# Moving the additions that build Winograd-style sums of weight blocks from VectorE to GpSimd

## The chip, the cores and the metric

The kernel runs on one core of one Trainium2 chip. The metric is the device time of one execution in microseconds (us). The profile names the engines PE (TensorE, matrix products), PEld (TensorE's weight loads), DVE (VectorE), ACT (ScalarE), POOL (GpSimd) and SP (SyncE, which issues nearly all DMAs). Each of them takes its instructions strictly in its own order; semaphores tell one engine that another is done.

## The reference

Random-feature attention, and behind it a two-layer network over all 4608 tokens, all in float32:

```
phi(x): h = x @ omega.T - |x|^2/2;  exp(h - max h) / sqrt(m)      # m = 128 features
kv = sum_s phi(k)[s] outer v[s];  z = sum_s phi(k)[s]             # for each of 8 batches, 8 heads
x  = (phi(q) @ kv) / (phi(q) . z + 1e-6)                          # 4608 tokens x 512
h  = x @ w_in;  g = h * tanh(softplus(h))                         # 512 x 2048
out = g @ w_out                                                   # 2048 x 512
```

## The kernel before

Matrix products run in float16. A float32 operand is kept as a high part (its cast to float16) and a low part (what the cast lost, again as float16), and three products (low by high, high by low, high by high) stand for one. The function `cast` (L71) makes a high part, `rest` (L80) a low part; a low part is one instruction that reads the float32 source and the high part, both from SBUF.

**The stages.** The tokens are worked in 18 chunks of 256. The attention for later tokens (`k_task`, `q_task`) is spread as small steps over the network's products for earlier chunks: an agenda hands out one step of each running task per slot, between groups of `ff_in` (x by w_in, tiles `ph`) and `ff_out` (g by w_out, tiles `po`). So PE gets a steady mixture of `ph`, `po`, `pk`/`pq` (features), `pkv` and `pn`.

**The sums.** The last three chunks (15 to 17, `ff_in7` and `ff_out7`) need seven products of blocks where the plain way needs eight. For that they use sums and differences of weight blocks, which `sums_make` (L797) prepares long before. It runs eight times: `t_make` four times for w_out (float32 scratch tile `sw`, results `t_w`, DRAM tiles `dt_w`), then `s_make` four times for w_in (scratch tile `s`, results also `s`, DRAM tiles `ds`). One call makes four results. Its ten additions and subtractions go through the local function `tt` (L805): two sums of blocks and a third that adds them, then result 1 is sent; two more, result 2 is sent; two more, result 3; three more, result 4. Each is 128x512 with a float32 output, and reads weight blocks in float16 or the scratch tile in float32. "Sent" (`send`, L808) is a cast on ACT, a low part on DVE and a DMA to DRAM. The fourth addition writes over the scratch that result 1's low part still reads, so it waits for that low part on DVE; likewise the eighth waits for that of result 2 and the ninth for that of result 3.

**What sets the order.** The agenda gives the order in which instructions are recorded; a scheduler then orders each engine's instructions by its own estimate of when they could start. So a change of engine moves neighbours too. What the prediction's steps touch, besides: the maximum of the features and its subtraction (L426, L435, DVE, out of PSUM), the exponential on ACT (L441, behind a table load), the cast and low part of `kp` and `qn` (ACT and DVE), the low part of `g` (L85, DVE), and on POOL the low parts `sk`, `sq` (of k and q), `vb` (of v) and `xs` (of x). `pkv` (L522) is the product on PE that reads `kp` and `vb`.

Of the kernel before, what the change touches and what calls it, by code (L numbers as in the profile page):

```python
# [30 lines left out]
def tile_kernel(  # L31
# [37 lines left out]
    act, dve, pool = nc.scalar, nc.vector, nc.gpsimd  # L69

    def cast(eng, out, in_, scale=1.0):  # L71

        if eng is act:
            act.activation(out, in_, AF.Copy, scale=scale)  # L74
        elif isinstance(scale, float) and scale == 1.0:
            eng.tensor_copy(out, in_)  # L76
        else:
            eng.tensor_scalar_mul(out, in_, scale)

    def rest(eng, out, in_, hi, scale=1.0):  # L80

        if isinstance(scale, float) and scale == 1.0:
            eng.tensor_tensor(out=out, in0=in_, in1=hi, op=ALU.subtract)  # L83
        else:
            eng.scalar_tensor_tensor(  # L85
                out=out, in0=in_, scalar=scale, in1=hi, op0=ALU.mult, op1=ALU.subtract
            )
# [177 lines left out]
    def did(*key):  # L265
        done[key] = done.get(key, 0) + 1

    def must(n, *key):
        assert done.get(key, 0) >= n, key
# [527 lines left out]
    def sums_make(key, blocks, first, shape):  # L797
        n = BW // 2
        must(1, "s", 0, NB - 1)
        must(1, "s", 1, 0)  # L800
        t = sb.tile([P, 2, n], F32, tag="ht", name=f"s{key[0]}_{key[1]}", bufs=HB)
        s, u = (t[:, i].rearrange("p (a b) -> p a b", a=shape) for i in range(2))
        b11, b12, b21, b22 = blocks

        def tt(out, in0, in1, op=ALU.subtract):  # L805
            dve.tensor_tensor(out=out, in0=in0, in1=in1, op=op)

        def send(op, src):  # L808
            o = sb.tile([P, 2, n], F16, tag="xs", name=f"{op}_{key[0]}_{key[1]}", bufs=2)
            cast(act, o[:, 0], src)  # L810
            yield 1
            rest(dve, o[:, 1], src, o[:, 0])
            sums[key[0], key[1], op] = dram.tile([P, 2, n], F16, name=f"d{op}_{key[0]}_{key[1]}")
            nc.sync.dma_start(out=sums[key[0], key[1], op], in_=o)
            yield 1

        ops = ("s1", "s2", "s4", "s3") if first is ALU.add else ("t1", "t2", "t4", "t3")
        tt(s, b22(0) if first is ALU.add else b12(0), b21(0) if first is ALU.add else b11(0), first)
        yield 1
        tt(u, b22(1) if first is ALU.add else b12(1), b21(1) if first is ALU.add else b11(1), first)  # L820
        yield 1
        tt(s, s, u, ALU.add)
        yield from send(ops[0], t[:, 0])
        if first is ALU.add:
            tt(s, s, b11(0))
            yield 1
            tt(s, s, b11(1))
        else:
            tt(s, b22(0), s)
            yield 1  # L830
            tt(s, s, b22(1), ALU.add)
        yield from send(ops[1], t[:, 0])
        last = b12 if first is ALU.add else b21
        tt(u, last(0), s)
        yield 1
        tt(u, u, last(1), ALU.add)
        yield from send(ops[2], t[:, 1])
        pair = (b11, b21) if first is ALU.add else (b22, b12)
        tt(s, pair[0](0), pair[1](0))
        yield 1  # L840
        tt(u, pair[0](1), pair[1](1))
        yield 1
        tt(s, s, u, ALU.add)
        yield from send(ops[3], t[:, 0])
        did("sums" if first is ALU.add else "tsums")
# [500 lines left out]
```

## Time and profile before

| | |
|---|---|
| time, median of 3 runs | 941.36 us (940.48 to 941.49) |
| the profiled execution's own time | 939.57 us |
| its span, first to last instruction | 937.8 us |
| mean granted TensorE clock | 0.993 |
| PE busy | 920.5 us (98%) |
| PEld busy | 689.4 us (74%) |
| DVE busy | 707.1 us (75%), 1234 instructions |
| ACT busy | 658.9 us (70%) |
| POOL busy | 213.6 us (23%), 134 instructions |
| DMA | 108.69 MB, mean 116 GB/s |
| the 80 instructions at L806 | 64.85 us on DVE, between 275 and 720 us |

A span is the time from the first to the last instruction; what lies around it in the profiled execution is 939.57 - 937.8 = 1.77 us. Busy time counts instructions that an engine executes; waiting before an instruction is not in it, but waiting inside one (for a port of the memory, say) is. In a timeline row the first number is the start in us from the span's beginning, the second the length in us, then engine, source line, operation, out<-in, shape and count; in brackets stands the engine's idle time before it and who ended it. A row that ends in x2 merges two instructions.

### The profile page before, as it was taken

The page shows a single profiled execution, that of the slowest core. Times are in us where ns is not written, and L with a number is a line of the kernel's source. Part 1 is how long each engine was busy: PE and PEld are TensorE (multiplying, and loading weights), DVE is VectorE, ACT ScalarE, POOL GpSimd, SP SyncE. Part 2 cuts the span into 40 slices and gives each one's busy share as a digit, 9 for nine tenths or more (in the row PEclk, how much of TensorE's full clock was granted, in tenths as well). Part 3 has the DMA queues.
Part 4 walks back from the last instruction along what each step waited for, and adds up shares of the span by engine and source line. Part 5 has one row for each costly group of instructions (what it writes and reads, how often), then busy time and mean ns, then how long its engine had stood idle before and what let it go on. Part 6 is the DMA issues. An engine that isn't in the chain of part 4 may idle for free. (4 is left out here: it accounts for less than half of the span.)

```text
span 937.8 us, 21111 instructions
## 1 busy us (share of the span) xinstructions
PE 920.5 (98%) x8795; PEld 689.4 (74%) x8795; DVE 707.1 (75%) x1234; ACT 658.9 (70%) x873; POOL 213.6 (23%) x134
## 2 busy tenths in 40 slices
PE   9799989999999999999999999999999999999998
PEld 6688765677777777777777777777777777679997
DVE  5799898685678688787688857878688756658774
ACT  6568966678777878778677776788786866345442
POOL 0000023242342224321333134231241232200000
PEclk9799999999999999999999999999999999999999
DMA  9766325443442256323543265523533156973521
GB/s 308 264 227 215 108 58 93 99 83 75 95 107 85 80 115 128 90 81 76 107 114 97 69 120 107 126 60 93 112 73 91 35 114 141 210 218 92 162 66 45
DMA packets 153055, 108.69 MB, mean 116 GB/s; under 512 B 112832, under 2 KB 125248, under 8 KB 152960
## 3 DMA queue, kind: packets, MB, share of 16 engines
q1 hardware_dynamic: 152640, 106.75, 44.6%
q8 instruction: 69, 1.13, 0.5%
q10 hardware_dynamic: 320, 0.59, 0.2%
q14 instruction: 26, 0.21, 0.1%
HBM read 63.14 MB, written 17.83 MB: 86 GB/s over the span
## 5 line engine op out<-in xcount | busy, mean ns | idle before, releaser
L770 PE MATMUL ph<-xT,w 128*128 128x256 f16 (+1 forms) x2816 | 342.2, 278 | 0.0
L1097 PE MATMUL po<-wo,g 128*128 128x512 f16 x1344 | 308.5, 379 | 0.0
L770 PEld LDWEIGHTS <-w 128*128 128x128 f16 x2688 | 260.7, 98 | 46.1 <-issue 0.6
L1097 PEld LDWEIGHTS <-g 128*128 128x128 f16 x1344 | 127.2, 98 | 132.7
L83 POOL TENSOR_TENSOR sq<-fq,sq 64x1024 f16<-64x1024 f32 x31 | 70.5, 2275 | 253.6 <-ACT sq L74 177.8
L955 ACT ACTIVATE h<-ph,us 128x512 f32<-128x512 f32 (+3 forms) x152 | 83.2, 573 | 49.7 <-PE ph L770 48.5
L85 DVE SCALAR_TENSOR_TENSOR g<-h,us,g 128x1024 f16<-128x1024 f32 (+3 forms) x76 | 99.9, 1325 | 15.2 <-ACT g L74 14.9
L83 POOL TENSOR_TENSOR sk<-fk,sk 64x1152 f16<-64x1152 f32 x24 | 59.3, 2469 | 91.6 <-ACT sk L74 79.3
L83 POOL TENSOR_TENSOR xs<-x,xs 128x512 f16<-128x512 f32 (+1 forms) x35 | 40.7, 1164 | 153.0 <-DVE xs L76 102.0
L955 ACT ACT_TABLE_LOAD x56 | 71.8, 1283 | 1.0
L441 ACT ACT_TABLE_LOAD x53 | 68.0, 1283 | 4.2 <-DVE ek L435 3.3
L426 DVE TENSOR_REDUCE mxq<-pq 128x4 f32<-128x512 f32 x72 | 46.7, 682 | 24.8 <-PE pq L401 23.9
L83 DVE TENSOR_TENSOR qn<-eq,qn 128x1024 f16<-128x1024 f32 x31 | 39.2, 1263 | 29.9 <-ACT qn L74 29.9
L906 PEld LDWEIGHTS <-w 128*128 128x128 f16 x1008 | 59.0, 98 | 3.3 <-issue 0.7
L441 ACT ACTIVATE ek<-ek,lnt 128x1152 f32<-128x1152 f32 x24 | 30.1, 1256 | 42.3 <-DVE ek L435 42.2
L74 ACT ACTIVATE g<-h,us 128x1024 f16<-128x1024 f32 (+3 forms) x64 | 58.2, 932 | 0.8
L426 DVE TENSOR_REDUCE mxk<-pk 128x4 f32<-128x512 f32 (+1 forms) x96 | 49.5, 546 | 7.3 <-PE pk L416 3.5
L83 DVE TENSOR_TENSOR kp<-ek,kp 128x1152 f16<-128x1152 f32 x24 | 32.8, 1366 | 27.0 <-ACT kp L74 26.2
L1044 PEld LDWEIGHTS <-gb 128*128 128x128 f16 x504 | 48.3, 98 | 5.2
L83 POOL TENSOR_TENSOR vb<-vf,vb 128x640 f16<-128x640 f32 x24 | 37.3, 1554 | 55.2 <-DVE vb L76 41.5
L955 ACT ACTIVATE h<-h,us 128x1024 f32<-128x1024 f32 (+2 forms) x16 | 14.7, 930 | 48.6 <-DVE h L915 48.6
L441 ACT ACTIVATE eq<-eq,lnt 128x1024 f32<-128x1024 f32 x31 | 35.6, 1149 | 18.8 <-DVE eq L435 18.5
(185 smaller groups left out, 1370.3 us busy)
## 6 DMA issues: line engine op xcount, KB each, us to landing
w<-ds SPq DMA_DIRECT2D x48, 256.0 KB, 3.6
vf<-in_vL_dram SPq DMA_DIRECT2D x32, 325.0 KB, 3.3
out_dram<-o SPq DMA_DIRECT2D x36, 256.0 KB, 2.3
fq<-in_qT_dram SPq DMA_DIRECT2D x31, 256.0 KB, 3.5
fk<-in_kT_dram SPq DMA_DIRECT2D x24, 256.0 KB, 3.6
raw<-in_w_out_dram SPq DMA_DIRECT2D x5, 1024.0 KB, 7.8
wo<-in_w_in_dram SPq DMA_DIRECT2D x4, 1024.0 KB, 10.6
raw<-in_w_in_dram SPq DMA_DIRECT2D x4, 1024.0 KB, 15.3
```

What stands on the lines that cost most here:

```text
L74: act.activation(out, in_, AF.Copy, scale=scale)
L83: eng.tensor_tensor(out=out, in0=in_, in1=hi, op=ALU.subtract)
L85: eng.scalar_tensor_tensor(out=out, in0=in_, scalar=scale, in1=hi, op0=ALU.mult, op1=ALU.subtract)
L426: sub = dve.tensor_reduce(out=mx[:, lo:hi], in_=pp[:, :m, :], axis=AX.X, op=ALU.max, negate=by_act)
L441: last = act.activation(e, e, AF.Exp, bias=lnt)
L770: nc.tensor.matmul(out=ph[:, i, :], lhsT=wi(a, k, f) if c else wi0(k, f), rhs=xT[c][:, y, k, :] if c else xT0()[:, k, :], start=n == 0, st ...
L906: nc.tensor.matmul(out=ph[:, i, :], lhsT=left(gr, op_l, i, a, k), rhs=x_region(c, r)[:, y, k0 + k, :], start=n == 0, stop=n == len(mm) - 1,)
L955: act.activation(h[:, :, lo:hi], ph[:, :, lo:hi], AF.Mish, scale=us[:, 0:1])
L1044: nc.tensor.matmul(out=ps, lhsT=gT[c, n][:, i, a, f, :], rhs=rhs, start=f == 0 and (a, y) == (1, 0), stop=f == FG - 1 and (a, y) == (0, 0),)
L1097: nc.tensor.matmul(out=po[i], lhsT=gT[c, gr][:, a, f % FG, i * P:(i + 1) * P], rhs=wo(y, f), start=f == 0 and (a, y) == parts[0], stop=f = ...
```

## The change

The ten additions and subtractions of each `sums_make` are issued to GpSimd instead of VectorE. Casts stay on ScalarE, low parts on VectorE, DMAs on SyncE's queue.

```diff
@@ sums_make
         def tt(out, in0, in1, op=ALU.subtract):
-            dve.tensor_tensor(out=out, in0=in0, in1=in1, op=op)
+            pool.tensor_tensor(out=out, in0=in0, in1=in1, op=op)
```

80 instructions leave DVE and 80 come to POOL. PE keeps its instructions in the same order; the other queues are reordered around the sums. The place shown here is the first call of `s_make` (scratch tile `s_0_6511`, made of weight slots `w_102` and `w_104`), about 512 to 550 us into the span. On POOL, between the low parts of v and of q, before and now in one (lines with + are new):

```order
 L83 TENSOR_TENSOR vb_116<-vf_3_5413,vb_116 128x10x64
+L806 TENSOR_TENSOR s_0_6511<-w_104 128x512 x2
+L806 TENSOR_TENSOR s_0_6511<-s_0_6511 128x512
+L806 TENSOR_TENSOR s_0_6511<-s_0_6511,w_102 128x512 x2
+L806 TENSOR_TENSOR s_0_6511<-w_102,s_0_6511 128x512
+L806 TENSOR_TENSOR s_0_6511<-s_0_6511,w_102 128x512
+L806 TENSOR_TENSOR s_0_6511<-w_102,w_104 128x512
 L83 TENSOR_TENSOR sq_6624<-fq_6509,sq_6624 64x1024
+L806 TENSOR_TENSOR s_0_6511<-w_102,w_104 128x512
+L806 TENSOR_TENSOR s_0_6511<-s_0_6511 128x512
 L83 TENSOR_TENSOR sq_6753<-fq_6667,sq_6753 64x1024
```

Eight sums stand ahead of the low part `sq_6624`, two behind it; the fourth, the eighth and the ninth each wait for a low part on DVE.

On DVE, in the same stretch (`s_0_0_6575` is result 1 of the call, `s_0_0_6683` result 2; `mxk_3` is the maximum for the k features of the fourth pair of heads, whose exponential becomes `kp_3`):

```order
-L806 TENSOR_TENSOR s_0_6511<-w_104 128x512
 L83 TENSOR_TENSOR kp_2_6343<-ek_2_6233,kp_2_6343 128x1152
-L806 TENSOR_TENSOR s_0_6511<-w_104 128x512
 L319 TENSOR_REDUCE vmx_8502<-vf_0_8366 128x1
-L806 TENSOR_TENSOR s_0_6511<-s_0_6511 128x512
 L83 TENSOR_TENSOR s_0_0_6575<-s_0_6511,s_0_0_6575 128x512
-L806 TENSOR_TENSOR s_0_6511<-s_0_6511,w_102 128x512
+L83 TENSOR_TENSOR s_0_0_6683<-s_0_6511,s_0_0_6683 128x512
 L426 TENSOR_REDUCE mxk_3_6399<-pk_3_0_6400 128x4
 L426 TENSOR_REDUCE mxk_3_6399<-pk_3_4_6409 128x1
```

The sums are gone, and the low part of result 2, which stood behind `kp_3` before, now stands ahead of `mxk_3`, right behind the low part of result 1.

On ACT, in the same stretch (`s_0_0_6846` is result 3; `ek_3` is the exponential, the line above it its table load):

```order
 L74 ACTIVATE s_0_0_6575<-s_0_6511 128x512
+L74 ACTIVATE s_0_0_6683<-s_0_6511 128x512
 L955 ACTIVATE h_0_0_6314<-ph_0_0_2_6373,us_6308 128x512
 L74 ACTIVATE g_0_6313<-h_0_0_6314,us_6308 128x1024
 L74 ACTIVATE sq_6624<-fq_6509 64x1024
+L74 ACTIVATE s_0_0_6846<-s_0_6511 128x512
 L74 ACTIVATE kv_5680<-pkv_2_6433 128x2x65
 L441 ACT_TABLE_LOAD
 L441 ACTIVATE ek_3_6398<-ek_3_6398,lnt 128x1152
+L74 ACTIVATE kp_3_6502<-ek_3_6398 128x1152
 L955 ACT_TABLE_LOAD
 L955 ACTIVATE h_0_1_6473<-ph_0_1_0_6474,us_6308 128x512
```

The casts of results 2 and 3 moved up, ahead of the exponential, and the cast `kp_3` now follows the exponential directly instead of standing behind the next table load.

## Prediction

> **What bounds the kernel now.** I read the page first: which engine is full.
>
> ```profile
> span 937.8 us, 21111 instructions
> ## 1 busy us (share of the span) xinstructions
> PE 920.5 (98%) x8795; PEld 689.4 (74%) x8795; DVE 707.1 (75%) x1234; ACT 658.9 (70%) x873; POOL 213.6 (23%) x134
> ```
>
> PE is busy for 920.5 of 937.8 us and no other engine for more than 75%. An average says little of the stretch in question, so the table by stretches comes next, with the cuts put where the sums (L806) begin and end.
>
> ```profile
> 0.00:275.00 275.00, 262.63 (x2161) 196.07 (x2162) 215.73 (x388) 204.34 (x315) 57.99 (x47) 0.98 0.54 147
> 275.00:720.00 445.00, 444.74 (x4215) 320.16 (x4214) 347.44 (x593) 339.29 (x403) 130.48 (x70) 1.00 0.40 96
> 720.00:938.00 218.00, 213.12 (x2423) 173.17 (x2421) 143.96 (x255) 115.32 (x156) 25.15 (x17) 1.00 0.46 118
> ```
>
> In 275 to 720 us PE is busy for 444.74 of 445.00 us at a full granted clock (1.00), while DVE is busy for 347.44 us (78%), ACT for 339.29 and POOL for 130.48 (29%). PE is the bound there and lacks 0.26 us. A view of waits says what PE waited for; this is its whole answer for PE's matrix products from 275 to 900 us, in us, times and longest.
>
> ```profile
> PE p_s L906 <- DVE h L915: 0.6, 1, 0.6
> PE pn L572 <- DMA qp<-qn: 0.5, 1, 0.5
> PE pn L572 <- DVE ek L435: 0.3, 1, 0.3
> ```
>
> 1.4 us in all, of which 0.3 lie before 720. One more wait is put down to PE's weight loads:
>
> ```profile
> PEld L522 <- DVE kp L83: 0.4, 1, 0.4
> ```
>
> So DVE's work between 275 and 720 us is not on the path that sets the end, except through such short waits. The change can gain next to nothing; what it can lose is the margin by which DVE, ACT and POOL run ahead of PE.
>
> **What is removed.** The sums on DVE, as a row of the table by stretches for L806 alone:
>
> ```profile
> 275.00:720.00 445.00, 64.85 (x80) 1.00 0.40 96
> ```
>
> 80 instructions, 64.85 us, all beside a busy PE: price on the path 0. DVE would come down to 347.44 - 64.85 = 282.6 us (64%). What an earlier DVE could win is PE's waits, 1.4 us at most or 0.15%, and most of these lie behind the last sum.
>
> **What is added.** 80 sums on POOL. No row has POOL read float16 blocks and write float32, so the nearest rows set the price: POOL's own two-input instructions, by size, mean ns of one behind the comma.
>
> ```profile
> L83 POOL TENSOR_TENSOR xs<-x,xs 128x512 f16<-128x512 f32 x32 | 38.4, 1200 | 140.2 <-DVE xs L76 89.2 <-issue 38.8 <-ACT xs L74 11.6
> L83 POOL TENSOR_TENSOR vb<-vf,vb 128x640 f16<-128x640 f32 x24 | 37.3, 1554 | 55.2 <-DVE vb L76 41.5 <-DVE rd L583 4.6 <-DVE vam L330 4.5
> L83 POOL TENSOR_TENSOR xs<-tt,xs 128x512 f16<-128x512 f32 x3 | 3.5, 1154 | 0.7 <-DVE xs L76 0.7
> L83 POOL TENSOR_TENSOR xs<-x,xs 128x256 f16<-128x256 f32 x3 | 2.3, 772 | 12.8 <-DVE xs L76 12.8
> ```
>
> 128x512 takes 1154 to 1200 ns; I take 1.15 us for a sum. Float16 inputs could make it cheaper, 0.77 us (the row with half the elements), or dearer, 1.55 us (a quarter more elements). 80 x 1.15 = 92 us bring POOL from 130.5 to 222.5 of 445 us, 50%: POOL does not become the bound.
>
> **What POOL and DVE do to each other.** Two pieces of the timeline. In the first a low part of `g` on DVE, with two inputs in SBUF, begins beside a low part on POOL:
>
> ```profile
> 495.72 2.37 POOL L83 TENSOR_TENSOR sk<-fk,sk 64x1152 f16<-64x1152 f32 x1 [6.46 <-ACT sk L74]
> 495.93 3.24 DVE L85 SCALAR_TENSOR_TENSOR g<-h,us,g 128x1024 f16<-128x1024 f32 x1
> ```
>
> POOL ends at 498.09; DVE's instruction ends 1.08 us later, at 499.17. It had stood still for 2.16 us. In the second DVE waits while POOL has more work ready:
>
> ```profile
> 577.99 1.34 POOL L83 TENSOR_TENSOR xs<-x,xs 128x512 f16<-128x512 f32 x1 [4.09 <-DVE xs L76]
> 578.24 0.80 DVE L319 TENSOR_REDUCE vmx<-vf 128x1 f32<-128x640 f32 x1
> 578.97 1.45 DVE L85 SCALAR_TENSOR_TENSOR g<-h,us,g 128x1024 f16<-128x1024 f32 x1
> ...
> 579.29 2.38 POOL L83 TENSOR_TENSOR vb<-vf,vb 128x640 f16<-128x640 f32 x1
> ```
>
> DVE's `g` (578.97) waits for the end of `xs` at 579.33 and ends at 580.42; `vb`, already begun, then needs until 581.67, 1.0 us longer than its mean. So the two take turns, a whole instruction each, and DVE waits for one POOL instruction at most. A sum on POOL thus costs a DVE instruction of that kind up to 1.15 us. If each of the 80 did, DVE would have 282.6 + 92 = 374.6 us, 84% of the stretch: dearer than now, and still not a bound. The Trainium skill, "Perfetto Trace Analysis", section on optimizing Scalar and DVE operations, speaks against the change: moving operations between these two engines might not help because they share a port. The rows agree that they block each other; by that rule the DVE relief would be smaller than 64.85 us, which the sum, with relief at 0, can do without.
>
> **What moves: the waits in line.** A queue in order can hold up work that has nothing to do with the sums. I looked for each call of `sums_make` at what stands between the results in the new order. In most calls DVE and ACT have work of their own between the results; in the last one the low part of result 4 stood ahead of the next maximum before too. I put these at 0; that is judged by the starts of their rows, not worked out for each. The first call of `s_make` is different: DVE's new order has the low part of result 2 directly behind that of result 1 and ahead of `mxk_3`. Between the two stand sums 4 and 5 on POOL and a cast on ACT, and DVE and ACT must wait for them. In the trace of before, POOL there:
>
> ```profile
> 511.45 1.41 POOL L83 TENSOR_TENSOR vb<-vf,vb 128x640 f16<-128x640 f32 x1 [2.23 <-DVE vb L76]
> 520.71 2.12 POOL L83 TENSOR_TENSOR sq<-fq,sq 64x1024 f16<-64x1024 f32 x1 [7.85 <-issue]
> ```
>
> DVE (maximum, subtraction, `g`, last subtraction, and the low part `kp` that PE wants):
>
> ```profile
> 517.91 0.69 DVE L83 TENSOR_TENSOR s<-s,s 128x512 f16<-128x512 f32 x1 [0.70 <-ACT s L74]
> 518.64 0.69 DVE L806 TENSOR_TENSOR s<-s,w 128x512 f32<-128x512 f32 x1
> 519.25 0.88 DVE L426 TENSOR_REDUCE mxk<-pk 128x4 f32<-128x512 f32 x2
> 520.05 0.88 DVE L435 TENSOR_TENSOR ek<-pk,mxk 128x512 f32<-128x512 f32 x2
> 520.84 0.68 DVE L426 TENSOR_REDUCE mxk<-pk 128x4 f32<-128x512 f32 x1
> 521.44 2.47 DVE L85 SCALAR_TENSOR_TENSOR g<-h,us,g 128x1024 f16<-128x1024 f32 x1
> 523.84 0.68 DVE L435 TENSOR_TENSOR ek<-pk,mxk 128x512 f32<-128x512 f32 x1
> ...
> 528.89 1.36 DVE L83 TENSOR_TENSOR kp<-ek,kp 128x1152 f16<-128x1152 f32 x1 [2.13 <-ACT kp L74]
> ```
>
> ACT (cast of result 1, exponential, cast of `kp`):
>
> ```profile
> 517.25 0.63 ACT L74 ACTIVATE s<-s 128x512 f16<-128x512 f32 x1 [1.84 <-DVE s L806]
> ...
> 524.55 1.26 ACT L441 ACTIVATE ek<-ek,lnt 128x1152 f32<-128x1152 f32 x1 [2.50 <-DVE ek L435]
> ...
> 527.71 1.15 ACT L74 ACTIVATE kp<-ek 128x1152 f16<-128x1152 f32 x1
> ```
>
> and PE's product, which needs `kp` complete (528.89 + 1.36 = 530.25), 0.81 us later:
>
> ```profile
> 531.06 1.12 PE L522 MATMUL pkv<-vb,kp 128*128 128x65 f16 x30
> ```
>
> Worked through with these lengths: `vb` ends at 512.86; three sums and one turn for DVE's `kp` of the heads before (1.36) end at 512.86 + 3.45 + 1.36 = 517.7, the cast 0.63 later at 518.3, the low part at 519.0 (before: 518.60). Sums 4 and 5 end at 521.3, the cast of result 2 at 521.9; its low part waits out sum 6 to 522.4 and ends at 523.1. Only then does `mxk_3` start, 3.9 us later than at 519.25. From it to `g` are 521.44 - 519.25 = 2.2 us: 525.3. `g` waits out sum 8 (525.4); `sq`, which held it until 522.83 before (1.4 of its 2.47 us), now comes behind it. It takes 1.1 more, and the last subtraction ends at 527.2, against 523.84 + 0.68 = 524.5. The exponential ends at 528.5, and the cast of `kp`, now directly behind, at 529.6 (before: 528.86). The low part of `kp` meets the low part of result 3 and the ninth sum; it ends between 531.0 (nothing in the way) and 531.9 (one sum, 1.15, in the way). PE wants it at 531.06. So PE waits 0 to 0.9 us; I take 0.7. With a sum of 0.77 us the wait is gone; with 1.55 us about seven sums on this way add 0.4 each, 2.8 us, and the wait is 3.5 us. The cover that hides all the rest is PE's backlog; where it is gone a late sum costs its lateness in full, but once, since while PE waits the others catch up.
>
> DMAs: each result's store to DRAM comes with its low part, a few us earlier or later in SyncE's queue; the results are read again some 100 us later or more, so 0.
>
> **Sum.** 0 for the removed work, 0 for the added, +0.7 for the one wait: 939.57 + 0.7 = 940.3 for the profiled execution. The runs' median stands 941.36 - 939.57 = 1.8 above that execution, so 942.1 is the forecast of the median. A difference below 0.2% (1.9 us) can hardly be told from none for this kernel: its own three runs spread over 0.1%.
>
> **The rivals.** First, slower: ACT and DVE stand in line behind POOL. The place is the stretch above, 517 to 532 us, and the price goes by the length of a sum: seven on the way, 0.7 us of wait at 1.15. To cost more than 1.9 us a sum must take (1.9 - 0.7) / 7 = 0.17 us more, 1.32 us. At 1.55 it costs 3.5 us: 944.9. For it: a `vb` of 128x640 already takes 1.55 on average, and DVE's turns lengthen the series. Against it: the rows with the sums' own shape lie at 1.15 to 1.20.
>
> Second, faster: the relief of DVE wins. DVE's `ek` and `kp` (rows above, 0.3 and 0.4) come earlier, since sums that stood ahead of them are gone. All 1.4 us gone gives 940.0, which is still no measurable change; for more, PE would have to run faster than it does, and no row shows room for that.
>
> Third, much slower: the work is simply on the worse engine. If every one of the eight calls makes PE wait for one whole sum, that is 8 x 1.15 = 9.2 us: 950.6. Against it: PE's margin in most calls is more than a sum. The Trainium skill, "GPSIMD Engine Reference", section on engine selection, sends elementwise additions to VectorE because GpSimd is about twice as slow for two inputs; the rows agree (64.85 / 80 = 0.81 us on DVE with its waits, 1.15 on POOL), but speed counts only where PE waits for it.
>
> **How the numbers follow.** The forecast has 0.62, the first rival 0.27, the second 0.07, the third 0.04. The second ends beyond 0.2% only if more than PE's known idle time goes: 0.03 for faster. Same is 0.62 + 0.04 = 0.66, slower 0.27 + 0.04 = 0.31. The range reaches down to the second rival, rounded to 940.1, and up past the first with 0.6 us for a second place of its kind, to 945.5.
>
> **What would show it.** Right: DVE busy some 40 to 65 us less and POOL some 92 more, L806 rows on POOL at about 1.15 us, PE still near 444 of 445 us in the stretch, and a wait of `pkv` for `kp` of under 1 us near 531. Wrong: waits of PE on `kp`, `ph`, `pn` or `po` of several us in sum between 275 and 720 (first or third rival), sums of 1.4 us or more, or ACT idle before casts of `s` and `t_w` for much longer than now with PE waiting behind it.

## The result and the profile after

The changed kernel takes 949.34 us (median of 4 runs, 947.55 to 951.95) against 940.92 us of the kernel before in the same comparison (4 runs, 938.77 to 941.49): a ratio of 1.0093, with a 95% interval of 1.0075 to 1.0111. It is slower by 0.9%, 8.4 us. The profiled execution took 948.67 us with a span of 946.9, 9.1 us more than that of before. The forecast was 942.1 us, with a range of 940.1 to 945.5.

The page's line of busy times, for the changed kernel:

```profile
PE 923.6 (98%) x8795; PEld 691.0 (73%) x8795; DVE 671.3 (71%) x1154; ACT 658.8 (70%) x873; POOL 329.5 (35%) x214
```

DVE lost 707.1 - 671.3 = 35.8 us of busy time and POOL gained 329.5 - 213.6 = 115.9, where 92 were forecast. The stretch of the sums in the table by stretches, with the same columns as before (busy time of PE, PEld, DVE, ACT and POOL, each with its number of instructions, then the granted clock, the DMA share and GB/s):

```profile
275.00:720.00 445.00, 440.57 (x4179) 317.51 (x4177) 305.35 (x505) 335.79 (x398) 240.87 (x148) 1.00 0.41 94
```

Between 275 and 720 us PE is idle for 4.43 us where it was idle for 0.26. And here is what PE's matrix products waited for from 275 to 900 us (us, times, longest):

```profile
PE pkv L522 <- DVE kp L83: 4.7, 3, 2.1
PE pk L401 <- DVE ek L435: 1.6, 1, 1.6
PE pn L572 <- DMA qp<-qn: 0.9, 1, 0.9
```

7.2 us instead of 1.4, in five places. So PE is the bound as before, and what hides the rest has holes. The sums themselves, first as the row of the table by stretches for L806 alone, then their largest group (shortest, median and longest in ns):

```profile
275.00:720.00 445.00, 111.24 (x79) 1.00 0.41 94
L806 POOL TENSOR_TENSOR sw<-wo x16: 1146/1242/2273, 275.2 to 498.3; 128x512 f32<-128x512 f16 x16
```

111.24 / 79 = 1.41 us on average: from 1.15 us, as forecast, with a median of 1.24 in this group, up to 2.27 where an instruction of DVE has to be let through (the sum at 287.54 below takes 2.15 us).

**Where the 9.1 us lie.** PE executes the same instructions in the same order in both kernels, so the lateness of one and the same product tells when time was lost. The first `pkv` product of five groups of heads, before:

```profile
197.85 1.12 PE L522 MATMUL pkv<-vb,kp 128*128 128x65 f16 x30
...
304.26 1.12 PE L522 MATMUL pkv<-vb,kp 128*128 128x65 f16 x30
...
427.56 1.12 PE L522 MATMUL pkv<-vb,kp 128*128 128x65 f16 x30
...
494.02 1.12 PE L522 MATMUL pkv<-vb,kp 128*128 128x65 f16 x30
...
725.75 1.13 PE L522 MATMUL pkv<-vb,kp 128*128 128x65 f16 x30
```

and after:

```profile
199.13 1.12 PE L522 MATMUL pkv<-vb,kp 128*128 128x65 f16 x30
...
308.16 1.00 PE L522 MATMUL pkv<-vb,kp 128*128 128x65 f16 x26 [0.69 <-DVE kp L83]
...
433.35 0.90 PE L522 MATMUL pkv<-vb,kp 128*128 128x65 f16 x13 [2.15 <-DVE kp L83]
...
501.29 1.12 PE L522 MATMUL pkv<-vb,kp 128*128 128x65 f16 x30
...
734.99 1.13 PE L522 MATMUL pkv<-vb,kp 128*128 128x65 f16 x30 [1.85 <-DVE kp L83]
```

The rows with x26 and x13 are cut off by the end of their view. The lateness is 1.28, 3.90, 5.79, 7.27 and 9.24 us. The first 1.28 lie ahead of the first sum: the profiled execution of before had begun quickly (in the ten other kernels' profiles below this product comes 0.72 to 2.25 us later than at 197.85). Then the first `t_make` costs 2.62 us. Before has a short wait near 381 (0.26 us of PE's idle time) that the changed kernel has not, which wins 0.43 us of lateness back, and the third `t_make` costs 2.31. Between 434 and 500 another 1.48 are lost with no wait: the granted clock fell behind that third place, told at the end. The last `s_make` costs 1.97. 1.28 + 2.62 - 0.43 + 2.31 + 1.48 + 1.97 = 9.23. The place that the prediction had worked through, the first `s_make`, costs nothing here.

**The first and the third `t_make`.** A timeline of the changed kernel in the first, put together from POOL, SyncE, DVE, ACT and PE in the order of time:

```profile
287.54 2.15 POOL L806 TENSOR_TENSOR sw<-sw,wo 128x512 f32<-128x512 f32 x1
289.66 1.40 POOL L83 TENSOR_TENSOR vb<-vf,vb 128x640 f16<-128x640 f32 x1
291.09 0.34 SPq L306 DMA_DIRECT2D vf<-in_vL_dram  x1
293.84 0.82 DVE L319 TENSOR_REDUCE vmx<-vf 128x1 f32<-128x640 f32 x1 [5.16 <-DMA vf<-in_vL_dram]
...
296.09 1.28 DVE L83 TENSOR_TENSOR t_w<-sw,t_w 128x512 f16<-128x512 f32 x2
...
300.88 0.63 ACT L74 ACTIVATE t_w<-sw 128x512 f16<-128x512 f32 x1 [8.15 <-POOL sw L806]
...
303.53 0.68 DVE L435 TENSOR_TENSOR ek<-pk,mxk 128x512 f32<-128x512 f32 x1
...
304.26 0.62 PE L401 MATMUL pk<-om,sk 128*128 128x128 f16 x8 [1.60 <-DVE ek L435]
```

and the rows of before that answer to them:

```profile
283.12 1.40 POOL L83 TENSOR_TENSOR vb<-vf,vb 128x640 f16<-128x640 f32 x1 [2.30 <-DVE vb L76]
284.55 0.34 SPq L306 DMA_DIRECT2D vf<-in_vL_dram  x1
287.20 0.82 DVE L319 TENSOR_REDUCE vmx<-vf 128x1 f32<-128x640 f32 x1 [1.34 <-DMA vf<-in_vL_dram]
...
291.68 0.63 ACT L74 ACTIVATE t_w<-sw 128x512 f16<-128x512 f32 x1 [2.35 <-issue]
...
295.98 0.68 DVE L435 TENSOR_TENSOR ek<-pk,mxk 128x512 f32<-128x512 f32 x1
```

Read down: four sums, the last of them at 287.54, stand on POOL ahead of the low part `vb`, which starts at 289.66 instead of 283.12 (1.28 of these 6.54 us are from before the first sum). `vb` is the last reader of a float32 tile `vf` (L305, five buffers), and the fetch of a later `vf` into that buffer waits for it: it is issued at 291.09, 0.03 us behind the end of `vb` (291.06), instead of 284.55. On DVE the maximum `vmx` over that fetch (L319) stands in line, though PE reads what is made of it only at 353.60. DVE is idle for 5.16 us in front of it, where it waited 1.34 before. Behind it stand two low parts `t_w`; POOL's last three sums wait for these; ACT's cast of the fourth result waits for the sums (8.15 us, at 300.88; in before the cast at this place of ACT's line is that of the second result, at 291.68), and the fourth result's low part stands on DVE ahead of the last subtraction `ek`, at 303.53 against 295.98; the exponential on ACT comes behind both. PE's backlog is used up: it waits 1.60 us for that subtraction and 0.69 us for `kp`. In the third `t_make` the same rows read 414.01 for `vb`, 415.44 for the fetch, 419.23 for `vmx` with an idle time of 6.20 us, and PE waits 2.15 us.

**The last `s_make`.** In the changed kernel the cast and the low part of result 4, and `kp`:

```profile
722.13 0.63 ACT L74 ACTIVATE s<-s 128x512 f16<-128x512 f32 x1 [3.62 <-POOL s L806]
722.80 1.21 DVE L83 TENSOR_TENSOR s<-s,s 128x512 f16<-128x512 f32 x1 [2.85 <-ACT s L74]
...
733.57 1.36 DVE L83 TENSOR_TENSOR kp<-ek,kp 128x1152 f16<-128x1152 f32 x1 [3.50 <-ACT kp L74]
```

and before:

```profile
713.56 1.07 DVE L83 TENSOR_TENSOR s<-s,s 128x512 f16<-128x512 f32 x1 [0.74 <-ACT s L74]
...
724.34 1.36 DVE L83 TENSOR_TENSOR kp<-ek,kp 128x1152 f16<-128x1152 f32 x1 [3.50 <-ACT kp L74]
```

The order on DVE is the same in both: the low part, the next maximum, `kp`. But the low part now ends a chain of POOL's sums, ACT's casts and DVE's low parts, and comes 9.24 us later. 7.27 of them PE is late itself. In before `kp` ended at 724.34 + 1.36 = 725.70, and PE used it at 725.75: there was no margin. So PE pays the remaining 9.24 - 7.27 = 1.97 us in full.

### The profile page after: what moved, and what is told of

It reads as the page before. It is cut to its first block, busy times and chain, and to the rows that moved or that the text cites. A ratio compares the mean times of both kernels' runs of the same rounds, so it can differ in the third digit from the quotient of the medians.

```text
span 946.9 us, 21117 instructions
## 1 busy us (share of the span) xinstructions
PE 923.6 (98%) x8795; PEld 691.0 (73%) x8795; DVE 671.3 (71%) x1154; ACT 658.8 (70%) x873; POOL 329.5 (35%) x214
## 5 line engine op out<-in xcount | busy, mean ns | idle before, releaser
L85 DVE SCALAR_TENSOR_TENSOR g<-h,us,g 128x1024 f16<-128x1024 f32 (+3 forms) x76 | 102.9, 1363 | 18.6 <-ACT g L74 18.4
L83 POOL TENSOR_TENSOR sk<-fk,sk 64x1152 f16<-64x1152 f32 x24 | 61.6, 2566 | 55.9 <-ACT sk L74 44.5
L83 DVE TENSOR_TENSOR qn<-eq,qn 128x1024 f16<-128x1024 f32 x31 | 42.4, 1366 | 35.3 <-ACT qn L74 35.3
L83 DVE TENSOR_TENSOR kp<-ek,kp 128x1152 f16<-128x1152 f32 x24 | 37.7, 1572 | 24.6 <-ACT kp L74 24.6
```

The costliest lines, as they stand in the source:

```text
L85: eng.scalar_tensor_tensor(out=out, in0=in_, scalar=scale, in1=hi, op0=ALU.mult, op1=ALU.subtract)
```

## The experiments

The theory formed from these rows was named the **late-fetch theory**, with a second place of its own at the last `s_make`. Its rivals: the **port theory** (POOL's sums hold up DVE's instructions, and the loss is spread over all of them), the **round-trip theory** (a result's way over three engines makes ACT and DVE stand in line, whatever the fetch), and the prediction's own (one place, the first `s_make`). The times of each set are compared with runs of the kernel before beside them, whose medians were 940.37, 940.28, 940.15 and 940.26 us.

The helper `behind(name)` in the diffs, which the kernel has already, queues what stands in its block behind the last instruction kept under that name, on the same engine and without a wait. TensorE's order is the same in all ten kernels.

**Which calls lose.** Two kernels divide the calls; the upper new line is the first, the lower the second.

```diff
-            pool.tensor_tensor(out=out, in0=in0, in1=in1, op=op)
+            (dve if first is ALU.add else pool).tensor_tensor(out=out, in0=in0, in1=in1, op=op)
+            (pool if first is ALU.add else dve).tensor_tensor(out=out, in0=in0, in1=in1, op=op)
```

The first kernel, with the sums of `t_make` alone on GpSimd:

> The sums of the four t_make calls on GpSimd, those of the four s_make calls on VectorE as before. Late-fetch theory (in the first and third t_make the sums stand ahead of the low part vb on GpSimd, which holds the buffer that the next vf is fetched into; VectorE's maximum vmx waits in order for that fetch, and the exponential and kp behind it come late): the places in these two calls stay, 1.8 + 0.9 us near 302 to 307 and 2.3 us near 431, and those after the s_make calls go: about 5 us over before, 945.9. Theory of the prediction (one place, the first s_make, and a place of that kind elsewhere only by chance): no more than before, 940.9. Port theory (every sum on GpSimd holds up VectorE, and the loss is spread over all sums): 44 of 80 sums stay, 8.4 x 44 / 80 = 4.6, 945.5, but spread over all four calls instead of two places.

Measured: 945.63 us (944.36 to 946.91), ratio 1.0053 (1.0041 to 1.0065), 5.3 us. PE's waits in its trace from 275 to 720 us are those of the two calls, 1.6 for `ek` and 2.6 for `kp`:

```profile
PE pkv L522 <- DVE kp L83: 2.6, 2, 1.9
PE pk L401 <- DVE ek L435: 1.6, 1, 1.6
```

The second kernel, with the sums of `s_make` alone on GpSimd:

> The reverse: the sums of the four s_make calls on GpSimd, those of t_make on VectorE. Late-fetch theory: what is left is the wait after the last s_make, about 2 us of kp near 728, and up to 1 us of pn near 792: 943.0 to 944.0. Theory of the prediction, with dearer sums of 1.3 to 1.4 us: PE waits for kp near 531, 2 to 3 us, and the whole loss is here, 949.3. Port theory: 36 of 80 sums, 8.4 x 36 / 80 = 3.8, 944.7, spread over the four calls.

Measured: 944.38 us (943.68 to 945.36), ratio 1.0039 (1.0027 to 1.0051), 4.0 us, a little above the 943.0 to 944.0 of the late-fetch theory. The two halves make 5.3 + 4.0 = 9.3 us. The wait behind the last `s_make` is there (1.86 us). Two others were not in the changed kernel's trace: one at the first `s_make`, and one that nothing had foretold:

```profile
533.46 1.13 PE L522 MATMUL pkv<-vb,kp 128*128 128x65 f16 x30 [0.48 <-DVE kp L83]
...
604.58 0.92 PE L572 MATMUL pn<-kv,qp 128*128 128x65 f16 x24 [1.72 <-DMA qp<-qn]
```

The first is the place of the prediction, at half a microsecond. In the changed kernel it is hidden: there `kp` is complete at 537.76, 4.36 us later than in this kernel, but PE comes to it at 538.33, 4.87 us later. The second is taken up below. The expectations count 44 sums for `t_make` and 36 for `s_make`; it is 40 each, which gives the port theory 4.2 us for either half. The two times, 5.3 and 4.0, do not refute it, but the places do: 4.2 of the 5.3 us are waits at two calls.

**Is it the fetch?** One kernel moves the maximum `vmx` alone.

```diff
-        yield 3 if b else 6
+        yield 3 + 1 * (b == 6) if b else 6
...
-            with behind(AV if b == 0 else None, 1):
+            with behind("dlo" if (b, hp) in ((4, 3), (6, 0)) else AV if b == 0 else None, 0 if b else 1):
...
-            yield 0 if hp % 2 == 0 or b == 0 else 1
+            yield 1 if (b, hp) == (4, 2) else 0 if (b, hp) in ((4, 3), (6, 1)) else 0 if hp % 2 == 0 or b == 0 else 1
...
-        anchors[nth] = (last.ins, sub.ins)
+        anchors[nth] = (last.ins, sub.ins); anchors["dlo"] = (sub.ins,)
```

`dlo` is the last subtraction of features that was written out. The shift by one step keeps that of the later steps.

> The changed kernel, with the maximum vmx of two fetches (the ones that VectorE waited for 5.2 us near 291 and 6.2 us near 413) queued some 50 places later on VectorE; TensorE's, ScalarE's, GpSimd's and SyncE's orders are the same, sums and low parts vb stay as late as they were. Late-fetch theory: VectorE goes on with the low parts, the exponential and kp come in time, and the 4.9 us of TensorE's waits at 302 to 307 and 431 go: 949.3 - 4.9 = 944.4. Round-trip theory (the casts and low parts of each result make ScalarE and VectorE stand in line behind GpSimd, whatever the fetch): not changed, 949.3. Port theory: not changed, 949.3.

Measured: 944.93 us (942.77 to 947.72), ratio 1.0050 (1.0034 to 1.0066): 4.4 us less than the changed kernel, 4.9 forecast. The fetch is issued as late as it was (SyncE, the first row), and yet PE waits in neither `t_make` (the second fence has all its waits from 275 to 900 us):

```profile
291.27 0.34 SPq L306 DMA_DIRECT2D vf<-in_vL_dram  x1
...
291.71 1.28 DVE L83 TENSOR_TENSOR t_w<-sw,t_w 128x512 f16<-128x512 f32 x2
```
```profile
PE pn L572 <- DMA qp<-qn: 2.2, 2, 1.8
PE pkv L522 <- DVE kp L83: 1.9, 1, 1.9
```

What is left of `pkv` is the last `s_make`, and `pn` is the unforetold wait near 600. The low parts `t_w` start at 291.71 instead of 296.09. The sums, the way of the results and the port are as in the changed kernel, so the round-trip and the port theory fall for these two calls: it is DVE's wait in line for the late fetch. The interval of this kernel and that of the change (1.0075 to 1.0111) do not meet.

**Is it the low part behind the sums?** One kernel moves POOL's line instead.

```diff
-            eng.tensor_tensor(out=out, in0=in_, in1=hi, op=ALU.subtract)
+            return eng.tensor_tensor(out=out, in0=in_, in1=hi, op=ALU.subtract)
...
-        rest(by("vlo", nth), v_lo, va, v_hi, s_v)
+        anchors["vlo"] = (rest(by("vlo", nth), v_lo, va, v_hi, s_v).ins,)
...
-            pool.tensor_tensor(out=out, in0=in0, in1=in1, op=op)
+            with behind("vlo"): pool.tensor_tensor(out=out, in0=in0, in1=in1, op=op)
```

> The changed kernel, with each sum of a weight block queued on GpSimd behind the last low part vb that was written out before it: in the first t_make vb then stands ahead of sums 4 to 7, in the third ahead of three of these four; TensorE's order is the same. Late-fetch theory: the fetch is issued as early as before, vmx does not wait, and 2.6 us of the first call and most of 2.3 of the third go: 944.4 to 945.5. Round-trip theory: the results' way from GpSimd over ScalarE and VectorE is as long in the third call as it was, so its 2.3 us stay and only the first call's may go: 946.7 to 949.3. Port theory: the same sums hold up VectorE as often, 949.3.

Measured: 943.01 us (941.41 to 946.36), ratio 1.0033 (1.0020 to 1.0045): 6.3 us less than the changed kernel, more than the 4 to 5 forecast (its profile has no wait near 600 and no fall of the clock either). In the first `t_make` `vb` stands ahead of sum 4 and `vmx` waits 0.47 us:

```profile
285.35 1.41 POOL L83 TENSOR_TENSOR vb<-vf,vb 128x640 f16<-128x640 f32 x1 [1.71 <-DVE vb L76]
...
289.57 0.82 DVE L319 TENSOR_REDUCE vmx<-vf 128x1 f32<-128x640 f32 x1 [0.47 <-DMA vf<-in_vL_dram]
```

In the third call the results go as long a way as before, with `vb` at 407.66 and a wait of 0.57 us for `vmx`, and PE waits nowhere. What is left of PE's waits for `kp` is that behind the last `s_make`:

```profile
PE pkv L522 <- DVE kp L83: 1.9, 1, 1.9
```

**The last `s_make`.** To the kernel just told, one more line, with the exponential's instruction kept under `exp`:

```diff
-            cast(act, o[:, 0], src)
+            with behind("exp" if op == "s3" and key == (1, 1) else None): cast(act, o[:, 0], src)
```

> The changed kernel with vb first, as in the run before, and the cast and the low part of the last result of the last s_make queued behind the next exponential on ScalarE and some 20 places later on VectorE; the sums and their order on GpSimd are the same. Theory of the line (this cast and low part come at the end of nine sums in a chain, 3.5 us later than on VectorE, and the maximum, the exponential and kp stand behind them): the wait of 2.0 us for kp near 727 goes, 943.0 - 2.0 = 941.0, that is the time of before within its spread. Port theory (the sums hold up VectorE itself): not changed, 943.0.

Measured: 941.86 us (939.04 to 943.80), ratio 1.0012 (0.9999 to 1.0024): no difference from before that the runs can tell, and 0.9 over the forecast (the turn told below is still open in this kernel). The median is 1.15 us under that of the fourth kernel, but the two intervals meet; what shows the place is the trace, in which no wait for `kp` is left. The sums on GpSimd are as they were, so here it is the line and not the port.

**Controls.** The sums of `t_make` alone, with the order behind `vb` of the fourth kernel:

> Only the sums of t_make on GpSimd, behind the low part vb; those of s_make on VectorE. Late-fetch theory: nothing is left of the 5.3 us that these calls cost with vb behind the sums: 940.4. Round-trip or port theory: 44 sums on GpSimd still cost 2 to 5 us: 942.4 to 945.6. Were the relief of VectorE worth anything (about 35 us less work), it would show here as a time under before, 939.5 or less.

Measured: 940.08 us (938.58 to 943.48), ratio 1.0001 (0.9991 to 1.0012). And the second and fourth `t_make` alone on GpSimd, with no order set:

```diff
+            (pool if key in (("w", 1), ("w", 3)) else dve).tensor_tensor(out=out, in0=in0, in1=in1, op=op)
```

> Only the sums of the second and the fourth t_make on GpSimd, the others on VectorE, with no order set by hand. Late-fetch theory: in these two calls no fetch that VectorE waits for hangs on a low part behind the sums, so nothing is lost: 940.4. Port theory: 22 of 80 sums, 8.4 x 22 / 80 = 2.3: 942.7. Round-trip theory: the results of these calls go the same way as those of the first and third, 2 to 3 us: 942.4 to 943.4.

Measured: 940.25 us (939.21 to 943.35), ratio 0.9999 (0.9991 to 1.0008). These 20 sums cost nothing, as the theory has it for calls in which no awaited fetch hangs on a low part behind them, though their results go the same way over three engines (for 20 sums, not 22, the port theory gives 2.1 us, which the interval excludes). PE's row between 275 and 720 us is full in both; the first is the kernel with all of `t_make`, the second that with two calls:

```profile
275.00:720.00 445.00, 445.00 (x4222) 320.79 (x4220) 327.51 (x554) 342.15 (x408) 189.17 (x111) 1.00 0.40 96
```
```profile
275.00:720.00 445.00, 445.00 (x4222) 320.75 (x4220) 337.36 (x574) 342.67 (x407) 159.74 (x91) 1.00 0.39 96
```

**The wait near 600.** In the second kernel it goes with a turn between DVE and POOL. DVE's low part `g` and POOL's `sk` start within 0.12 us of each other:

```profile
587.60 2.36 POOL L83 TENSOR_TENSOR sk<-fk,sk 64x1152 f16<-64x1152 f32 x1 [3.92 <-issue]
587.72 3.32 DVE L85 SCALAR_TENSOR_TENSOR g<-h,us,g 128x1024 f16<-128x1024 f32 x1
```

`g` came second and took 3.32 us, and what stands behind it on DVE, up to the low part `qn` that PE's `pn` needs by way of `qp`, is late. Two more kernels have the sums of `s_make` alone on GpSimd. In one only the very last result is moved, as above:

> Only the sums of s_make on GpSimd, with the cast and the low part of the very last result queued behind the next exponential (as in the run that did this to the changed kernel). Theory of the line: the 2.0 us of kp near 728 go, those of pn near 603 (1.9) and of kp near 533 (0.65) stay: 944.4 - 2.0 = 942.4. Port theory: not changed, 944.4.

Measured: 942.73 us (940.26 to 944.76), ratio 1.0020 (1.0009 to 1.0031). The median is where it was forecast, but the profiled execution, 941.26 us, has no wait near 603. The order on each engine at this place is that of the second kernel; this time `g` won the turn, by 0.16 us, and `sk` waited:

```profile
587.18 1.28 DVE L85 SCALAR_TENSOR_TENSOR g<-h,us,g 128x1024 f16<-128x1024 f32 x1
587.34 3.35 POOL L83 TENSOR_TENSOR sk<-fk,sk 64x1152 f16<-64x1152 f32 x1 [3.93 <-DVE vmx L319]
```

Six of the profiles have this order, with `g` and `sk` 0.03 to 0.16 us apart. In two `g` comes second, and PE waits 1.72 us (second kernel) and 1.77 us (third). In four it comes first, and PE waits nowhere near 600: the changed kernel, the fourth, the fifth and this one. Of the eleven times of this kernel six lie above 942.5 us, of the twelve of the next one two; this suggests that one program goes either way from execution to execution, but no two traces of one program show it. The other kernel queues the maximum ahead of `g` later, so that `g` can start well ahead of `sk`:

```diff
-            with behind(AV if b == 0 else None, 1):
+            with behind("dlo" if (b, hp) == (7, 2) else AV if b == 0 else None, 0 if b else 1):
```

> As the kernel before it, and the maximum vmx that VectorE waits for 5.0 us near 582 queued some 80 places later, so that the low part g that stood behind it starts ahead of GpSimd's low part sk and need not stand still behind it (g took 3.32 us there, against 1.27 where it came first). If that lost turn makes the wait of 1.9 us for qp near 603: 942.4 - 1.9 = 940.5, and g takes about 1.3 us. If it is the results' way over three engines in the second s_make: the wait stays, 942.4.

Measured: 940.58 us (939.83 to 942.72), ratio 1.0009 (1.0000 to 1.0018), and `g` took 1.44 us at 580.59, 5.65 us ahead of `sk`. This edit also takes `g` out from behind DVE's wait of 5.0 us for a fetch. That this wait alone is not the cause is shown by the six profiles: DVE waits 4.7 to 5.0 us there in all of them.

**All of it together**: the changed kernel, all 80 sums on GpSimd, with these three orders.

> All 80 sums on GpSimd as in the changed kernel, with the three orders of the runs before together: sums behind vb, the very last result behind the next exponential, and the maximum vmx near 582 queued later. If these three places and the first s_make's half microsecond are the whole of the loss: 940.2 + 0.6 - 0.4 (TensorE's own wait near 381, which went in most of the other runs) = 940.4, no difference from before, and TensorE busy for 445 of 445 us. If 80 sums on GpSimd cost something more that the runs of parts did not show: 942 or more. If the relief of VectorE by 36 us of busy time can bring something once nothing waits: under 938.3.

Measured: 940.10 us (939.18 to 944.50), ratio 1.0007 (0.9996 to 1.0018). Its stretch, and all of PE's waits to 900 us:

```profile
275.00:720.00 445.00, 445.00 (x4220) 320.49 (x4218) 314.02 (x513) 342.56 (x406) 246.64 (x150) 1.00 0.41 95
```
```profile
PE pn L572 <- DMA qp<-qn: 0.3, 1, 0.3
PE p_s L906 <- DVE h L915: 0.2, 1, 0.2
```

As far as the runs can tell (the interval ends at 0.18%, 1.7 us), the places of these three orders are the whole of the loss. Nor does PE wait at the first `s_make`: `kp` is complete at 530.83 and PE comes at 531.34. DVE's relief brings nothing that the runs can tell, even with these waits gone. None of the ten kernels is faster than the one before.

## Why the prediction was wrong

**What was right.** PE is the bound; the relief of DVE is worth 0 (last experiment: DVE busy for 674.3 us instead of 707.1, and no time won). 80 sums on POOL need not cost anything by themselves. Most sums alone take what the nearest row said, 1.15 us (1.26 where both inputs lie in the scratch tile). POOL and DVE take turns by whole instructions: the rows near 587 us above show both outcomes, with 3.32 us for the loser in one profile (`g`) and 3.35 us in the other (`sk`). The Trainium skill, "SBUF — State Buffer", section on SBUF's two separate sides, describes this as an exclusive lock that whoever starts first holds for the whole instruction, and these rows agree. DVE's busy time in the whole run fell by 35.8 us and not by the 64.85 that left it: its other instructions became 29 us longer together. The place that was worked out was also sized rightly: 0.7 us forecast at the first `s_make`, 0.48 measured in the second kernel, where nothing ahead of it had cost PE time. This was not luck, for the steps in between fit as well: from the start of `vb` to that of `mxk_3` the working has 523.1 - 511.45 = 11.65 us, and the second kernel and the changed one both take 11.66; to the end of `kp` it has 19.6 to 20.5, and they take 20.2. It did not show in the change itself because PE was late by then: "while PE waits the others catch up".

**The step that failed** is this one: "In most calls DVE and ACT have work of their own between the results; in the last one the low part of result 4 stood ahead of the next maximum before too. I put these at 0; that is judged by the starts of their rows, not worked out for each." Three of the other seven calls were not 0 but 2.62, 2.31 and 1.97 us, and the fall of the clock behind the second of these three cost 1.48 more in the profiled execution. For the last call the observation itself was right and the conclusion wrong. That an instruction already stood ahead of the maximum says nothing for the cover when that instruction becomes later; the new chain of sums, casts and low parts in front of it had to be added up as was done for the first `s_make`.

For the two `t_make` calls the reason lies in a link that the prediction left out. "DMAs: each result's store to DRAM comes with its low part, a few us earlier or later in SyncE's queue; [...] so 0" speaks of the DMAs of the moved step alone (and of the reading of the results 100 us later, which does not hold for all: in before the first `w<-ds` is issued at 520.64, 2.01 us behind the first store; no loss in the runs hangs on it). But the sums were also put ahead of `vb` on POOL, and `vb` sets free the buffer of a fetch. With that the fetch came 6.5 us later (291.09 against 284.55). The link itself could be seen in before's trace: the fetch at 284.55 follows the end of `vb` (283.12 + 1.40 = 284.52) by 0.03 us, and DVE waited in line for such fetches already, 14.0 us in 9 times between 275 and 720 us, before a `vmx`. A low part was followed to its product only, not to the buffer that it reads.

"DVE waits for one POOL instruction at most" fits the rows here (`g`: 3.32 us instead of 1.28, beside 2.36 us of `sk`), but it was priced only where the sums themselves stand. The turn near 587 us is between two instructions that are no sums at all, set side by side by the new order of DVE.

Three slips of the working change nothing in this: `vb` at 579.29 is 2.38 - 1.55 = 0.83 us longer than its mean, not 1.0; the upper end for `kp` is 531.0 + 1.15 = 532.1, not 531.9; and the range's lower end, 940.1, lies above the second rival's 940.0.

**The rivals.** The first (longer sums) has its condition met on average, 1.41 us, but the mean is raised by the turns. By its own rule that would be 0.7 + 7 x (1.41 - 1.15) = 2.5 us at the first `s_make`; the place costs nothing in the changed kernel and 0.48 us in the second, so it is not the cause. The third came nearest with its number, 950.6, with the wrong mechanism: not a sum's length at each of eight calls, but three places, and five calls at nothing or half a microsecond. For the second, no kernel shows a gain: the last experiment has DVE's relief and no waits, and is not faster. The "wrong" signs that the prediction named are the ones that came: waits of PE for `kp` of several us, sums of 1.4 us on average, and ACT idle ahead of the casts of `s` and `t_w`.

The rule of the Trainium skill, "GPSIMD Engine Reference", section on engine selection, that additions of two inputs belong on VectorE, gave the right advice. The rows agree that GpSimd is the slower (1.41 us against 64.85 / 80 = 0.81, 1.7 times), but the loss did not come from the speed: with another order the same 80 slower instructions cost nothing.

## What to carry to other kernels

When a step moves to another engine's queue, follow every instruction that it now stands ahead of to all that waits for it: its product, and also the buffer that it reads and the next fetch into that buffer. An instruction that waits in line for a late fetch holds up everything behind it, even where its own result is wanted much later; so queue it where its data is surely there. Where an idle engine's work is hidden by a backlog, work out each place at which the backlog could run out, not one.

## What the runs showed of the hardware that was not expected

A wait of PE cost more than its length in one case. In the changed kernel PE waited 2.15 us up to 433.35, and the granted clock (third number from the end) was low in the stretches around and behind that:

```profile
432.00:436.00 4.00, 2.65 (x35) 2.39 (x36) 2.17 (x2) 3.96 (x5) 0.00 (x0) 0.65 0.02 4
436.00:440.00 4.00, 4.00 (x29) 2.78 (x27) 2.79 (x5) 3.05 (x4) 2.13 (x1) 0.92 0.00 0
```

0.65 and 0.92, with 1.48 us lost between the products at 433.35 and 501.29. It shows in the products themselves: the `pkv` group at 433.35 takes 1.83 us instead of 1.12, the `ph` group behind it 3.59 instead of 2.78. In the kernel with `t_make` alone the same place has a wait of 1.9 us and the clock stays at 1.00; so it does behind the waits of 1.60 and 1.85 us in the changed kernel, and behind those of 1.72 and 1.77 us near 600. The Trainium skill, "TensorE: Matmul & The Clock Gate", section on what is actually happening, says that the clock is throttled after an idle window of about 3.4 us that runs freely. The wait here, 2.15 us, is shorter than that, and yet the fall came behind it. It is the longest of the waits named; whether its length decides or the moment at which it falls was not tried. Such falls also come and go ahead of any sum: between 130 and 145 us PE is busy for 13.1 us in all twelve profiles, and the clock is 0.89 in three of them (the second, fifth and sixth of the ten kernels) and 1.00 in the other nine.
